# Attention and gated experts on one core: another way through the first 256 tokens of batch 0

## The chip, the cores and the metric

The kernel runs on one core of a Trainium2 chip. Its engines work in parallel, each through its own queue in order: PE (TensorE, matrix products and transposes), DVE (VectorE), ACT (ScalarE), POOL (GpSimd) and SP (SyncE, which here issues nearly all DMAs). The metric is the device time of one execution in microseconds, as the median of several runs.

## What is computed

Eight batches of 576 tokens go through a windowed attention with 8 heads of 64, and the result through a layer of four experts that are attention heads themselves.

```python
rel = pos[:, None] - pos[None, :]
mask = (rel >= 0) & (rel < 128)
scores = np.where(mask, q @ k.T / 8 - slope[h] * abs(rel), -1e9)   # per batch and head
x = softmax(scores) @ v                                            # (8, 576, 512)
...
logits = x @ w_gate                                                # 4 experts, the best 2 are kept
for e in range(4):
    q, k, v = x @ wq[e], x @ wk[e], x @ wv[e]                      # 512 -> 64
    ye = softmax(causal(q @ k.T / 8)) @ v @ wo[e]
    out += (weight of e per token, 0 if not among the best 2) * ye
```

## The kernel before

The heads are taken two at a time: a pair has 128 rows, head 0 of the pair in partitions 0 to 63 and head 1 in 64 to 127. In batch 0 the pairs are called g = 0 to 3. A key block is 128 keys wide, and since the window is 128, a block of 128 queries sees its own key block and the one ahead of it.

**Wrapped scores.** For query block i the kernel computes 256 scores per query (`products`), of which the mask leaves exactly 128, and folds them: where a key of the own block lies in the future, the score of the same column in the block ahead is copied over it (`wrap`, COPY_PREDICATED on DVE with the mask `mkt`). The softmax then works on 128 columns (`softmax_block` on DVE, shown as CUSTOM_DVE_ANT_0 or ISA; `exp_block` on ACT; `normalise` by `scl`, on POOL or ACT). After the transposes on PE, `split` (DVE, TENSOR_TENSOR with `tmt`) spreads the 128 columns again over two key blocks, one masked out for each entry, and PE multiplies by the values (`half_pv`).

**Batch 0 in halves.** The first batch is the start of the program, where nothing else is to be done. Its pairs are therefore worked in halves: half A (`x == 0`) is query blocks 0 and 1 of each pair, half B is blocks 2 and 3 and, by `half_tail`, the last 64 tokens. `half_s` makes scores and softmax, `half_t` the transposes, `half_pv` the product with the values. It leaves each x in two parts, `xh` (rounded to the type that PE takes in one pass) and `xl` (what the rounding left), in the tiles `wx`. `fetch(g, m, x)` brings only the part of q and k that a half needs, in pieces of 64 partitions x 2 x 256 (128 KB), the rest for half B later with other sources (`rd`).

**Weights.** `wload(c)` fetches 128x772 of the joined weights, `wprep(c)` rounds them into `WH` and puts the rest into `WL`. Every projection (`qkproj`, `vproj`) is the sum of three products for each of four pairs: WH by xh, WH by xl, WL by xh.

**What sets the order.** The whole program is first recorded as a list. `plan` then puts it in the order that the table `ORDER` gives, a long compressed string of numbers, and `nc.any` leaves the table the choice between two engines for copies, roundings and scalings. `place` gives out the buffers by that order: eight PSUM banks `ps`, and in SBUF eight of `w5` (w50 to w57), three of `w10` (w100 to w102) and four of `w4` (w40 to w43). An engine works its queue strictly in order, so an instruction that waits holds up all that stand behind it on the same engine. All compute instructions come from one line, L1189.

Of the kernel before, what the change touches and what calls it, by code (L numbers as in the profile page):

```python
# [10 lines left out]
F32 = mybir.dt.float32  # L11
# [9 lines left out]
DM = H * D  # L21
# [9 lines left out]
BIG = 3.0e38  # L31
EPS = 1e-9
# [6 lines left out]
    "c-p;KeOO#sdB69bckVgKy_*?3v(C6PEBMS*Xc<c?bfFFvTIT7{9onHn1q&8jMnfAOVI35@ObZH?C_IHND7cB6)I>p{5*sSG@RU@dpu{B=Y_N$2g{NSHCKf"  # L39
    "6vY18-Id*=f-Yd`+z<zw#Lk8|GhzQ6bP{@x>q!mqqZIPsVeKYrOmGCYuFQ>%z-v8K{;h(b;Yo><!;<0MQmKgl4wblhq4x~Nh`ed(9xr+Q%|MU6nTiZGR#Z"  # L40
    "7iPxD*~#vIGGwEmPQ9aSsJs_AHUGCP}W}wETDQ)B1~=}&#Lq+yHpktsz@cXQCc6ORm?4aWJCUU#^8l_?ziudJWAZ&%sn)ub$`b*yz8`8vE}BG_JdXMusb-"
    "_LvrcPz*^=+Q*-n*tX%E31QzE??nQ6G{A6)p0ono+`TqQ}Ebzd4q>QgW$6oi`u@mcWhYz0rG9~OWcR>__Q?}BcE`VH^%wa7NJGh{}*LNcb#r-hQI1SJXD@"
    "%}@?-z19r}`|)!^OPGw!CwtMR=M;m~9H0ak(c!JI+!UovE;8Qk%nE&~$#}qJ^-D@_XKeIcEO^yc0qmfHeLfEn-&HM;FW!aB&3Y7=Q{z&=o4{^;Sb2^*IYX"
    "h1AJXoq1V#R<OIki7)M@tD(HCAYo>h@M!b3;N$_Afl2<`F?Myi+*PzQVqx=nFdQllK$hRvGwhnZUo(6;pjecd6JL7ZyleHW`qQW_)#vX9#Y0n$KjVM?qvh"
    "=ohWOD1XFBlLQu{|A*l7v*=m;a!#uT;zA%K4MDn7EeR8cbSFAliQ6xvevp%9<|^8I)tIL_YwsSo!3=DR+e>8F+9YSxbzRSI60O6}loQQOS7F0-58e(pX0q"
    "*AJy5g{3`{l<28O?Hbh`?}AcHxM)BBJ6FS>$Y`wo{yw5=LjKor=K=QoB2JGH$DL&5^)6V#ACJCQ=R9QW?a?9S87rr&Ff@smNQOv4P6V0y1r%g%vS(Z!b@)"
    "-4-buoVe-H#{}HQ!X|<%3%#1fwltLK}dZ!itH9@2#2z9mfZh%xL`j{%zqOj`#a{v!J+v*zBsnEHZxkBB@+9t&^WMNijv8p!OpK^Qd!j+jt!ft=(yEo6lbv"
    "TXBECd~maBX(9X>53Gtv*n^1);J~ruKTo^6=96hhYmupyp-|X(MdS`|D4+gBQ*YncL5%V^-RGm^(zRRTSuZ|8Ub6of@Cm+s8Mvl<1eg6meA`Lgq_T0hV9_"
    "Hem~6jW_XxkG`}5=g&-6=fZ{)!Of55ryl$KXIEFVa<lReKxrb)JJ-qT;=<QfM}H64!M@|MFJAe?r!3h4wSc|mgj&j)x`w{$Gj*E5Y&ENdq+1Gsdc4pB{X_"
    "le+$w<4>tW(v7=);+cH_=gv@KXx)!-<8ph3O%EMbhWE||h^v)2p#BtY1`-ZQmM$I5(5_sXW)<fWd`e&%H5iY<D6<oubuP*&7;al2z~f2VE@SS5SYQ`xo;z"  # L50
# [192 lines left out]
def attn_moe_kernel(ctx, tc, hd, rd, vd, wall, wo, mk, tb, tm, mt, ident, out):  # L243
# [1033 lines left out]
```

## Time and profile before

| | us |
|---|---|
| median of 3 runs | 477.76 (477.13 to 478.05) |
| the profiled execution | 478.22 |
| its span, first to last instruction | 476.4 |
| PE busy | 468.2 (98%) |
| DVE busy | 410.3 (86%) |
| ACT busy | 371.0 (78%) |
| POOL busy | 218.2 (46%) |

The ends of matrix products are modelled, so that PE is shown busy also where its products follow each other loosely. The mean granted clock of PE is 0.996; it was lower only between 10 and 15 us, at 0.66. Of the chain of work that ended last, PE holds 80% of the span, DVE 8%, DMA 4%, ACT 3%.

### The profile page before, as it was taken

The numbers are of one execution on the slowest core, as the hardware profiler recorded it, in microseconds if no ns is written. First come the engines' busy times: TensorE is split into PE (matmuls) and PEld (weight loads), VectorE is DVE, ScalarE is ACT, GpSimd is POOL, SyncE is SP. The second block draws the span as 40 slices with busy tenths as digits, with TensorE's granted clock in tenths as the row PEclk, the third lists the DMA queues.
The fourth block names the chain that finished last, engine by engine and source line by source line (L and its number), as shares of the span: only waits on it lengthen the run. The fifth ranks groups of instructions, "written<-read, shape, count | busy, mean of one in ns | idle before, by whom it ended". The sixth has DMA issues, their size and how long they took to land.

```text
span 476.4 us, 17537 instructions
## 1 busy us (share of the span) xinstructions
PE 468.2 (98%) x6380; PEld 409.5 (86%) x6380; DVE 410.3 (86%) x1900; ACT 371.0 (78%) x1416; POOL 218.2 (46%) x451
## 2 busy tenths in 40 slices
PE   7999999999999999999999999999999999999996
PEld 5888889897889788798898988998889897899875
DVE  6899999989998998879979898898998979975840
ACT  5867978978989577797987989498786968934962
POOL 4713779093826227243381626625163613352440
PEclk9899999999999999999999999999999999999999
DMA  8889333009136026160362047411733030300033
GB/s 200 263 206 225 89 110 80 7 2 221 49 104 141 2 68 192 34 161 1 87 174 68 1 116 192 119 27 38 167 94 102 4 85 2 119 1 1 3 111 111
DMA packets 29861, 44.98 MB, mean 94 GB/s; under 512 B 9424, under 2 KB 15824, under 8 KB 29776
## 3 DMA queue, kind: packets, MB, share of 16 engines
q1 hardware_dynamic: 29040, 43.42, 34.3%
q8 instruction: 50, 0.82, 0.7%
q10 hardware_dynamic: 736, 0.46, 0.4%
q14 instruction: 35, 0.29, 0.2%
HBM read 34.42 MB, written 9.44 MB: 92 GB/s over the span
## 4 chain that ended last, share of the span: by engine, by line
PE 80%; DVE 8%; DMA 4%; ACT 3%; SPq 2%; POOL 2%; issue 1%; DVEq 0%
PE ps L1189 80%; DVE w L1189 5%; ACT w L1189 2%; SPq L1189 2%; POOL w L1189 2%; DMA w<-in_hd 2%; DMA w<-in_rd 1%; DVE ps L1189 1%; DMA w<-in_wall 1%; DVE KKm L1189 0%; DVE r L1189 0%; DVE WL L1189 0%; DVE ALm L1189 0%; DVE mr L1189 0%; ACT QJm L1189 0%
## 5 line engine op out<-in xcount | busy, mean ns | idle before, releaser
L1189 ACT COPY w<-ps 128x512 f32<-128x512 f32 (+3 forms) x230 | 92.9, 449 | 31.1 <-PE ps L1189 20.1
L1189 PE MATMUL ps<-wx,WH 128*128 128x288 f32 (+2 forms) x512 | 110.6, 300 | 0.0
L1189 ACT ACTIVATE w<-w,nm 128x128 f32<-128x128 f32 x252 | 98.8, 395 | 7.5 <-DVE nm L1189 7.3
L1189 POOL TENSOR_SCALAR w<-w,r 128x128 f32<-128x128 f32 x165 | 60.6, 380 | 88.5 <-ACT w L1189 30.5
L1189 POOL TENSOR_SCALAR w<-w,mr,w 128x256 f32<-128x256 f32 (+3 forms) x128 | 78.2, 621 | 43.0 <-DVE mr L1189 15.8
L1189 PEld LDWEIGHTS ps<-wx,WH 128*128 128x128 f32 x512 | 83.3, 189 | 1.5 <-DVE mnm L1189 0.2
L1189 ACT ACTIVATE w<-w,mnm 128x256 f32<-128x256 f32 (+3 forms) x128 | 70.9, 557 | 14.4 <-DVE mnm L1189 13.0
L1189 DVE CUSTOM_DVE_ANT_0 w<-ps,tbt 128x128 f32<-128x128 f32 x288 | 72.5, 283 | 2.9 <-PE ps L1189 2.1
L1189 DVE TENSOR_TENSOR w<-ps,tmt 128x768 f32<-128x768 f32 (+3 forms) x96 | 72.4, 771 | 2.0 <-PE ps L1189 0.9
L1189 PE MATMUL ps<-wx,WL 128*128 128x288 f32 (+2 forms) x256 | 72.0, 296 | 0.0
L1189 PE MATMUL ps<-WH,wx 128*128 128x260 f32 x288 | 62.9, 287 | 0.0
L1189 PE MATMUL ps<-idt,w 64*128 64x64 f32 (+1 forms) x1152 | 60.4, 231 | 1.3 <-POOL w L1189 1.0
L1189 PE MATMUL ps<-w 64*64 64x192 f32 (+3 forms) x1256 | 58.9, 306 | 0.5 <-DMA w<-in_hd 0.4
L1189 PEld LDWEIGHTS ps<-idt,w 64*128 64x128 f32 (+1 forms) x1152 | 48.1, 139 | 11.4 <-issue 3.7
L1189 PE MATMUL ps<-w,vt 64*64 64x192 f32 (+4 forms) x1344 | 56.6, 284 | 0.4 <-ACT w L1189 0.4
L1189 PEld LDWEIGHTS ps<-w,vt 64*64 64x64 f32 (+1 forms) x1344 | 49.7, 133 | 6.5 <-ACT w L1189 1.0
L1189 DVE COPY_PREDICATED ps<-mkt,ps 128x128 f32<-128x128 int32 (+2 forms) x160 | 50.0, 329 | 2.4 <-PE ps L1189 2.0
L1189 PEld LDWEIGHTS ps<-w 64*64 64x64 f32 (+1 forms) x1256 | 45.0, 134 | 7.8 <-DMA w<-in_hd 1.6
L1189 DVE CUSTOM_DVE_ANT_0 w<-ps,mtt 128x384 f32<-128x384 f32 (+2 forms) x96 | 49.8, 551 | 1.0 <-PE ps L1189 0.6
L1189 PEld LDWEIGHTS ps<-WH,wx 128*128 128x128 f32 x288 | 48.4, 190 | 0.7 <-DVE nm L1189 0.2
L1189 PE MATMUL ps<-w,w 128*64 128x64 f32 (+4 forms) x576 | 48.2, 319 | 0.0
L1189 ACT ACTIVATION_READ_ACCUMULATOR w<-w,nm 128x1 f32 x252 | 48.2, 191 | 0.0
(110 smaller groups left out, 944.9 us busy)
## 6 DMA issues: line engine op xcount, KB each, us to landing
w<-in_hd SPq DMA_DIRECT2D x56, 288.0 KB, 4.7
vt<-in_vd SPq DMA_DIRECT2D x28, 320.0 KB, 4.3
out<-w SPq DMA_DIRECT2D x31, 256.0 KB, 2.7
w<-in_hd SPq DMA_DIRECT2D x14, 128.0 KB, 3.6
w<-in_hd SPq DMA_DIRECT2D x56, 32.0 KB, 3.9
w<-in_wall SPq DMA_DIRECT2D x4, 386.0 KB, 5.5
out<-w SPq DMA_DIRECT2D x8, 128.0 KB, 2.3
vt<-in_vd SPq DMA_DIRECT2D x4, 192.0 KB, 4.8
```

The source lines that it names most:

```text
L1189: getattr(getattr(tc.nc, e), m)(*a, **k)
```

## The change

- **Fetches.** Each pair of batch 0 now comes in two DMAs of 64 partitions x 1216 (304 KB each), q and k whole for both halves; the first pair's second one is issued by ACT. `rd` is no longer read. `tmt` and the low part of `mkt` move from ACT's queue to SP's, behind weights and values. The tail's q comes by `fetch_tl`, one 128x128 DMA for each pair.
- **Half A without wrap.** `first_blocks` gives query block 0 its 128 scores and block 1 all its 256, side by side. The softmax of block 1 runs over 256 columns, there is no COPY_PREDICATED and no `split`. The bias for it is a new table FT, made at the start by two instructions on DVE and four on POOL, in the memory of the tile `KKm`, which is free until the first key projection. The three blocks of each head are transposed (6 instead of 4 transposes per pair) and copied out by two copies of 128x384.
- **Weights.** `wprep` rounds and subtracts in two pieces, 512 and 260 columns. The products with `WL` come last in the first projections (`terms`).
- **Tail scores of the batches after the first.** The two 64x128 and the two 64x64 products trade their rows; the fold then goes into the other bank. The number of instructions is the same.
- **A new `ORDER`** for the whole program. Counted over the program: PE 4794 instructions before, 4800 after; DVE 1902 and 1891; ACT 976 and 963; POOL 456 and 485; SP 241 and 238.

```diff
-    "c-p;KeOO#sdB69bckVgKy_*?3v(C6PEBMS*Xc<c?bfFFvTIT7{9onHn1q&8jMnfAOVI35@ObZH?C_IHND7cB6)I>p{5*sSG@RU@dpu{B=Y_N$2g{NSHCKf"
...
+    def fetch(g):
+        if g % 2 == 0:
+            raws["e", g // 2] = big10.tile([P, 2 * (QW + S)], F32, tag="e", name=f"e{g}")
+        z = (QW + S) * (g % 2)
+        e = raws["e", g // 2][:, z : z + QW + S]
+        a = hd[0, NP_ - 1 - g]
+        nc.sync.dma_start(e[:D], a[:D, : QW + S])
+        (nc.sync if g else nc.scalar).dma_start(e[D:], a[D:, QW + S + P :])
+        raws[g] = ([e[:, : NQ * P], e[:, P:QW]], e[:, QW:])
...
+    def first_blocks(g, ss, q, k, tb):
+        nm, sm, pt = state[g, 0]
+        for i in range(2):
+            n = P + P * i
+            for h in range(2):
+                d = slice(D * h, D * h + D)
+                for y in range(2):
+                    m = P * i + D * y
+                    nc.tensor.matmul(
+                        ss[h][D * y : D * y + D, P * i : P * i + n], q[h][d, m : m + D], k[d, :n], start=True, stop=True
+                    )
+        for h in range(2):
+            for i in range(2):
+                c = 2 * h + i
+                a = ss[h][:, : 3 * P].rearrange("p (a n) -> p a n", n=P)[:, i : 2 * i + 1, :]
+                v = pt[:, 3 * h + i : 3 * h + 2 * i + 1, :]
+                bias = tb[:, h, 1 - i :, :].bitcast(F32)
+                softmax_block(a, v, bias, nm[:, c : c + 1], P + P * i)
+                exp_block(None, v, nm[:, c : c + 1], sm[:, c, 0:1], P + P * i)
...
         if x == 0:
-            evac(w[:, : 4 * P].rearrange("p (h n) -> p h n", h=2)[:, :, :P], t[:, 0:2, :], 2 * P)
-            split(diag_pair(w, 1, 1, P), t[:, 2:4, :], P)
...
+            for h in range(2):
+                t = ps_t.tile([P, 4, P], F32, tag="t", name=f"tA{g}_{h}")
+                for k in range(3):
+                    nc.tensor.transpose(t[:, k, :], pt[:, 3 * h + k, :], idt)
+                evac(w[:, 3 * P * h : 3 * P * h + 3 * P].rearrange("p (a n) -> p a n", n=P), t[:, :3, :])
...
+    def terms(late):
+        return sorted(((c, j) for c in range(4) for j in range(3)), key=lambda z: late and z[1] == 2)
...
-            for lhs, rhs in ((WH, xh), (WH, xl), (WL, xh)):
...
+            lhs, rhs = ((WH, xh), (WH, xl), (WL, xh))[j]
...
+            for f in (slice(0, 4 * P), slice(4 * P, NW)):
+                w, hi, lo = wst[c][:, f], WH[:, NP_ - 1 - c, f], WL[:, NP_ - 1 - c, f]
+                rnd(hi, w)
+                ssub(lo, w, hi.bitcast(F32))
...
+    nc.vector.tensor_scalar(FT[:, 3, :, 0, :], tbt[:, 3, 0:3:2], -1.0e6, NEG, op0=ALU.is_ge, op1=mul)
+    nc.vector.tensor_tensor(FT[:, 3, :, 0, :], FT[:, 3, :, 0, :].bitcast(F32), tbt[:, 3, 1:4:2], add)
+    nc.gpsimd.tensor_scalar(FT[:, 3, :, 1, :], tbt[:, 3, 0:3:2], 1.0, 0.0, op0=mul, op1=add)
+    for p in (2, 1, 0):
+        nc.gpsimd.tensor_scalar(FT[:, p], FT[:, 3].bitcast(F32), float(4 ** (3 - p)), 0.0, op0=mul, op1=add)
```

The order on SP at the start of the program. `w100` holds pairs 0 and 1, `w101` pairs 2 and 3; `in_wall` are the weights, `in_vd` the values. Before:

```order
L1189 DMA w100_90<-in_hd 64x2x256 x4
L1189 DMA w101_91<-in_hd 64x2x256 x4
L1189 DMA w100_90<-in_hd 128x2x128
L1189 DMA w100_90<-in_rd 128x2x320
L1189 DMA w100_90<-in_hd 64x2x256 x2
L1189 DMA w51_83<-in_wall 128x772
L1189 DMA vt0_128<-in_vd 128x256
L1189 DMA vt1_129<-in_vd 128x256
L1189 DMA w55_87<-in_wall 128x772
L1189 DMA vt2_130<-in_vd 128x256
L1189 DMA vt3_131<-in_vd 128x256
```

The same place now (ACT issues one more 64x1216 for w100 beside it):

```order
L1189 DMA w100_90<-in_hd 64x1216 x3
L1189 DMA w101_91<-in_hd 64x1216 x2
L1189 DMA w51_83<-in_wall 128x772
L1189 DMA w101_91<-in_hd 64x1216 x2
L1189 DMA vt0_128<-in_vd 128x256
L1189 DMA w52_84<-in_hd 128x128
L1189 DMA vt1_129<-in_vd 128x256
L1189 DMA w53_85<-in_hd 128x128
L1189 DMA mkt_107<-in_mk 128x64
L1189 DMA w54_86<-in_wall 128x772
L1189 DMA vt2_130<-in_vd 128x256
L1189 DMA vt3_131<-in_vd 128x256
```

Before, the half A of all four pairs (eight pieces of 128 KB) and four DMAs for half B of pairs 0 and 1 stood ahead of the first weights; now the whole rows of pairs 0 to 2 do, pair 3 follows the first weights, and all values stand behind pair 3.

The order on DVE, from the last blocks of pair 2 in half A (`nmA2`) to the first of pair 3 (`nmA3`); `nm` names the pair and half of a softmax block, KKm is the table FT. Before:

```order
L1189 TENSOR_REDUCE r1_0_135<-sm1_116 128x4
L1189 RECIPROCAL r1_0_135<-r1_0_135 128x4
L1189 ISA w52_84,nmA2_136<-ps4_73,tbt_108 128x128
L1189 ISA nmA2_136 128x1
L1189 COPY_PREDICATED ps5_74<-mkt_107,ps5_74 128x128
L1189 ISA w52_84,nmA3_138<-ps5_74,tbt_108 128x128
L1189 ISA nmA3_138 128x1
L1189 COPY_PREDICATED ps6_75<-mkt_107,ps6_75 128x128
L1189 ISA w52_84,nmA3_138<-ps5_74,tbt_108 128x128
```

The same place now:

```order
L1189 TENSOR_REDUCE r1_0_135<-sm1_116 128x4
L1189 ISA w57_89,nmA2_136<-ps6_75,KKm_125 128x128
L1189 ISA nmA2_136 128x1
L1189 COPY_PREDICATED ps4_73<-mkt_107,ps4_73 128x2x128
L1189 RECIPROCAL r1_0_135<-r1_0_135 128x4
L1189 COPY_PREDICATED ps5_74<-mkt_107,ps5_74 128x2x128
L1189 TENSOR_TENSOR WL_112<-w51_83,WH_111 128x512
L1189 ISA w50_82,nmA3_138<-ps7_76,KKm_125 128x256
L1189 ISA nmA3_138 128x1
L1189 TENSOR_REDUCE r2_0_137<-sm0_115 128x4
L1189 ISA w50_82,nmA3_138<-ps7_76,KKm_125 128x128
```

Between the two pairs there now stand three COPY_PREDICATED for half B of pairs 0 and 1 and a subtraction for WL; pair 3's blocks of half A stand ahead of every softmax block of half B (`tbt` in place of KKm), which follow a few rows later.

The order on POOL from the scalings of pair 2's half A to the last part of WL. Before:

```order
L1189 TENSOR_SCALAR w52_84<-w52_84,r2_0_137 128x128 x2
L1189 TENSOR_SCALAR w52_84<-w52_84,r3_0_139 128x128
L1189 TENSOR_SCALAR w52_84<-w52_84,r2_0_137 128x128
L1189 TENSOR_SCALAR WH_111<-w51_83 128x772
L1189 TENSOR_TENSOR WL_112<-w51_83,WH_111 128x772
L1189 TENSOR_SCALAR WH_111<-w55_87 128x772
L1189 TENSOR_TENSOR WL_112<-w55_87,WH_111 128x772
L1189 TENSOR_SCALAR w53_85<-w53_85,r0_4_141 128x128
L1189 TENSOR_SCALAR WH_111<-w56_88 128x772
L1189 TENSOR_SCALAR w54_86<-w54_86,r1_4_143 128x128
L1189 TENSOR_SCALAR WH_111<-w57_89 128x772
```

The same place now (`r0_4` and `r1_4` are half B of pairs 0 and 1; w51, w54 and w57 hold the raw weights):

```order
L1189 TENSOR_SCALAR w50_82<-w50_82,r3_0_139 128x128
L1189 TENSOR_SCALAR w50_82<-w50_82,r3_0_139 128x256
L1189 TENSOR_SCALAR WH_111<-w54_86 128x512
L1189 TENSOR_SCALAR WH_111<-w54_86 128x260
L1189 TENSOR_TENSOR WL_112<-w54_86,WH_111 128x512
L1189 TENSOR_SCALAR w52_84<-w52_84,r0_4_141 128x128 x4
L1189 TENSOR_SCALAR WH_111<-w51_83 128x512
L1189 TENSOR_TENSOR WL_112<-w51_83,WH_111 128x512
L1189 TENSOR_SCALAR w53_85<-w53_85,r1_4_143 128x128 x4
L1189 TENSOR_TENSOR WL_112<-w57_89,WH_111 128x512
L1189 TENSOR_TENSOR WL_112<-w51_83,WH_111 128x260
L1189 TENSOR_TENSOR WL_112<-w57_89,WH_111 128x260
```

Before, POOL made two of the four WL and DVE the other two; now POOL makes three of the four 512-wide pieces, the last two of them each behind four scalings of half B, and three of the four 260-wide ones.

## Rows read from the trace of the kernel before

**Rows 1.** Stretches of 20 us: PE, PEld, DVE, ACT, POOL busy (instructions), clock, DMA share, GB/s
```profile
0.00:20.00 20.00, 17.39 (x161) 13.47 (x161) 14.39 (x92) 13.07 (x55) 11.62 (x24) 0.91 0.92 254
20.00:40.00 20.00, 19.83 (x240) 17.15 (x238) 19.39 (x87) 13.43 (x60) 6.36 (x14) 1.00 0.80 192
40.00:60.00 20.00, 19.95 (x330) 17.61 (x329) 19.35 (x100) 17.92 (x80) 11.46 (x24) 1.00 0.59 146
...
420.00:440.00 20.00, 20.00 (x189) 19.79 (x189) 11.52 (x46) 6.14 (x20) 8.58 (x20) 1.00 0.00 1
```

**Rows 2.** Chain that ended last, in order of time: start us, us, what
```profile
25.02 26.80 PE ps L1189 x380
51.83 0.27 ACT w L1189
...
65.29 0.28 ACT w L1189
...
66.17 43.24 PE ps L1189 x626
```

**Rows 3.** Timeline of the first 28 us: start, us, engine, operation [idle before, releaser]
```profile
4.80 0.90 PE L1189 MATMUL ps<-w 64*64 64x192 f32 x16
...
8.72 0.52 PEld L1189 LDWEIGHTS ps<-w 64*64 64x64 f32 x12 [0.37 <-DMA w<-in_hd]
...
18.37 0.38 PE L1189 MATMUL ps<-WH,wx 128*128 128x260 f32 x1
...
22.80 0.71 DVE L1189 TENSOR_TENSOR wx<-ps,wx 128x256 fp32r<-128x256 f32 x2
23.43 1.53 DVE L1189 TENSOR_TENSOR WL<-w,WH 128x772 fp32r<-128x772 f32 x1
...
25.02 0.50 PE L1189 MATMUL ps<-WL,wx 128*128 128x260 f32 x2 [0.17 <-DVE WL L1189]
...
27.37 0.49 PE L1189 MATMUL ps<-w 128*128 128x192 f32 x2
```

**Rows 4.** Instructions on DVE in the first 70 us, by form: count | busy us, mean ns
```profile
L1189 DVE CUSTOM_DVE_ANT_0 w<-ps,tbt 128x128 f32<-128x128 f32 x72 | 17.4, 281 | 2.3 <-PE ps L1189 2.1
...
L1189 DVE TENSOR_TENSOR w<-ps,tmt 128x1024 f32<-128x1024 f32 x4 | 4.9, 1216 | 0.0
L1189 DVE COPY_PREDICATED ps<-mkt,ps 128x128 f32<-128x128 int32 x16 | 4.3, 288 | 0.3 <-PE ps L1189 0.3
...
L1189 DVE TENSOR_TENSOR w<-ps,tmt 128x512 f32<-128x512 f32 x4 | 2.7, 683 | 0.4 <-ACT w L1189 0.4
L1189 DVE TENSOR_TENSOR WL<-w,WH 128x772 fp32r<-128x772 f32 x2 | 2.5, 1238 | 0.0
...
L1189 DVE CUSTOM_DVE_ANT_0 w<-ps,mtt 128x256 f32<-128x256 f32 x2 | 0.8, 422 | 0.0
```

**Rows 5.** Stretches: the last two numbers are the DMA engines' busy share and GB/s
```profile
1.00:2.00 1.00, 0.70 (x3) 0.70 (x4) 1.00 (x6) 0.00 (x0) 0.25 (x1) 1.00 0.27 41
...
3.00:9.00 6.00, 5.58 (x69) 3.98 (x70) 3.32 (x27) 3.85 (x14) 2.20 (x3) 1.00 1.04 222
15.00:18.00 3.00, 3.00 (x44) 2.26 (x38) 2.20 (x13) 1.85 (x9) 2.92 (x4) 1.00 1.03 379
109.00:116.00 7.00, 7.00 (x126) 5.27 (x126) 7.00 (x28) 5.26 (x21) 3.69 (x4) 1.00 1.05 242
```

**Rows 6.** DMA issues: queue, operation xcount, KB each, median us from issue to landing
```profile
w<-in_hd SPq DMA_DIRECT2D x14, 128.0 KB, 3.6
...
w<-in_wall SPq DMA_DIRECT2D x4, 386.0 KB, 5.5
...
tbt<-in_tb ACTq DMA_DIRECT2D x1, 160.0 KB, 2.5
```

**Rows 7.** Timeline of POOL at the start: start, us, operation [idle before, releaser]
```profile
9.05 2.83 POOL L1189 TENSOR_SCALAR w<-w,r 128x128 f32<-128x128 f32 x8 [3.42 <-DVE nmA L1189]
...
15.38 0.83 POOL L1189 TENSOR_SCALAR WH<-w 128x772 fp32r<-128x772 f32 x1
16.29 1.83 POOL L1189 TENSOR_TENSOR WL<-w,WH 128x772 fp32r<-128x772 f32 x1
```

More of the change, by code (lines that the diff above doesn't have):

```diff
@@ L31 @@
 BIG = 3.0e38
+NEG = -8.0e9
 EPS = 1e-9
@@ L499, in half_s, with first_norm @@
             ss = [ps_s.tile([P, 512], F32, tag="s", name=f"s{'AB'[x]}{g}_{h}") for h in range(2)]
-        part = products(ss, 2 * x, [q, q], k, tbt[:, p], 2, 5 * x)
+        if x == 0:
+            first_blocks(g, ss, q, k, FT[:, NP_ - 1 - g])
+            return
+        part = products(ss, 2, q, k, tb, 2, 5)
         for h in range(2):
-            wrap(ss[h], 2 * x)
-            blocks((g, x), ss[h], part[h])
+            wrap(ss[h], 2)
+            blocks((g, 1), ss[h], part[h])
+    def first_blocks(g, ss, q, k, tb):
[17 more added lines that the diff above has]
+                exp_block(None, v, nm[:, c : c + 1], sm[:, c, 0:1], P + P * i)
+    def first_norm(g):
+        nm, sm, pt = state[g, 0]
+        r = p2.tile([P, 5], F32, tag="r", name=f"r{g}_0", bufs=3)[:, :4]
+        nc.vector.tensor_reduce(r, sm[:, 0:4, :], AX.X, add)
+        nc.vector.reciprocal(r, r)
+        for c in range(4):
+            h, i = divmod(c, 2)
+            v = pt[:, 3 * h + i : 3 * h + 2 * i + 1, :]
+            scl(v, v, r[:, c : c + 1])
     def half_tail(g):
         s = ps_a.tile([P, 512], F32, tag="a", name=f"sC{g}")
-        nc.tensor.matmul(s[:, :TW], *prepped[g][4][2:4], start=True, stop=True)
+        nc.tensor.matmul(s[:, :TW], half["p", g][:, 0, :], prepped[g][4][1][:, S - TW :], start=True, stop=True)
         nc.vector.copy_predicated(s[:, 0:TAIL], mkt[:, P:], s[:, P:TW])
@@ L739, in qkproj @@
         o = acc[:, :n]
-        k = 0
-        for c in range(4):
+        for k, (c, j) in enumerate(terms(b == 0 and half == 0)):
             xh, xl = xT[4 * b + c]
             cw = c if b else NP_ - 1 - c
-            for lhs, rhs in ((WH, xh), (WH, xl), (WL, xh)):
-                nc.tensor.matmul(
-                    o, lhs[:, cw, P * mtile : P * (mtile + 1)], rhs[:, n0:n1], start=(k == 0), stop=(k == 11)
-                )
-                k += 1
+            lhs, rhs = ((WH, xh), (WH, xl), (WL, xh))[j]
+            nc.tensor.matmul(
+                o, lhs[:, cw, P * mtile : P * (mtile + 1)], rhs[:, n0:n1], start=(k == 0), stop=(k == 11)
+            )
         sl = slice(n0, n1)
@@ L1102, in attn_moe_kernel @@
     warm()
-    fetch(1, 1, 0)
+    for g in range(1, 4):
+        fetch(g)
     fetch_v(0, 0)
-    fetch(2, 2, 0)
     fetch_v(1, 0)
+    wload(0)
     fetch_v(2, 0)
-    wload(0)
     fetch_v(3, 0)
```

279 lines of the change are left out of this document (114 added, 165 removed).

## The prediction

> **What bounds the kernel now.** I read the stretches of 20 us first, then the chain, then the timeline of the start, where the change lies. Between 20 and 60 us DVE is busy 19.39 and 19.35 of 20 us, while PE, shown as busy, has its products less densely: in 420 to 440 us DVE needs only 11.52 of 20 us and PE's weight loads fill 19.79, against 17.15 and 17.61 [rows 1]. So in the first 60 us DVE is as good as full, and later PE is. The chain says the same with a seam: it runs on PE from 25.02 us, leaves it at 51.83 us for ACT and DVE until 65.6 us (13.8 us), and returns to PE at 66.17 us [rows 2]. What the start costs, DVE decides together with what arrives when: scores begin at 4.80 us, the last pair's half A at 8.72 us, the first projection at 18.37 us; the last two `xl` leave DVE at 22.80 to 23.51 us, DVE then makes WL from 23.43 us on, PE waits for it at 25.02 us, and these projections end at 27.37 us [rows 3]. After that PE always has something to do. So the change can gain in two ways: an earlier end of this first part, and less DVE work in the part up to 65 us.
>
> **DVE's work.** Out go eight COPY_PREDICATED 128x128 of 0.288 us (2.3 us), four `split` 128x512 of 0.683 us (2.7 us), and two WL of 772 columns, 1.238 us each (2.5 us), for which one piece of 512 and one of 260 come back: as many columns as one, 1.2 us. In come eight softmax blocks of 256 columns in place of 128: 8 x (0.422 - 0.281) = 1.1 us; three of the eight copies 128x384, between 0.42 us (256 columns) and 0.68 us (512), say 0.55 us: 1.7 us; two instructions for FT over 256 columns, 0.8 us. Sum: -2.3 - 2.7 - 1.3 + 1.1 + 1.7 + 0.8 = **-2.7 us** of DVE time [rows 4]. Its other copies trade engines in the new order by less than 1 us net. PE gets eight more transposes and 16 wider products, under 1 us, all in the first 20 us, where it waits anyway; ACT gets eight exponentials of twice the width and five of the copies, and has room there (busy 13.07 and 13.43 of 20 us [rows 1]).
>
> **The fetches.** A whole pair is two pieces of 304 KB where half A needed two of 128 KB. What rate do they get? In 3 to 9 us, when the 64-partition pieces of 1 KB rows came in, the DMA engines were fully busy at 222 GB/s; in 15 to 18 us, mostly weights over 128 partitions, they moved 379 GB/s; in 109 to 116 us, where the large pieces are 64 partitions again, with rows of 2.3 and 4.6 KB, 242 GB/s [rows 5]. Long rows therefore don't help; the number of partitions goes with the rate, and I take 242. [...]
>
> Ahead of pair 3's scores lie the table of 160 KB, the identity (128x128, 64 KB), eight pieces of 64x1216 (304 KB each; 2656 KB in all, 2.72 MB) and one weight piece of 386 KB [rows 6]. Data flows from about 2 us: in 1 to 2 us the DMA engines are busy 0.27 [rows 5]. 2.72 MB at 242 GB/s are 11.2 us, the weights at 379 another 1.0 us: pair 3 lands at **14.3 us**, and the first values 0.4 us later. At 222 it is 15.3 us, at 379 it would be 10.2 us. Before, the last scores of half A began at 8.72 us. So the whole-row fetch itself makes half A later, not earlier; pairs 0 and 1 have their half B scores in exchange.
>
> **The first part, after pair 3.** DVE's queue holds every half-B block behind pair 3's blocks. From these to the last `xl` DVE has: 2 blocks of 256 and 13 of 128 (4.5 us), three copies (1.7), four subtractions and two casts of 256 (2.5), a `split` of 256 (0.4), a WL of 260 (0.4), some nine small ones (1.6): 11.1 us. Neighbours overlap: two subtractions of 0.42 us take 0.71 us together [rows 3], so of 34 instructions about 2 us go off. 14.3 + 9.1 gives 23.4 us for the last `xl`; before it was 23.51. DVE then stands even on the x, but has already done what it did before up to about 26 us (no WL, no second half of the weights), which is the 2.7 us above.
>
> Now the end of the projections. DVE makes pair 1's half-B sums only after a `split` of 128x1024, 1.22 us [rows 4], so near 25.0 us. POOL then has four scalings (8 in 2.83 us, 1.4 us) and the last WL of 512 (1.83 us x 512 / 772 = 1.2 us) [rows 7]: 27.6 us, and four products follow on PE: **28.1 us** where before it was 27.4. By then PE has also made the half-B scores of pairs 2 and 3 and more transposes, but fewer projections; about the same work: 19 projections of 256 to 260 columns less, against 16 score products of 192 in two passes (two side by side), two tails and five transposes. So this part costs 0.7 us; with pair 3 one us earlier or later, between -1.5 and +2 us.
>
> **After it.** DVE is ahead by 2.7 - 0.7 = 2.0 us of its old place. What of it the end sees: nothing, if PE alone decided between 28 and 65 us; all, if DVE did. DVE is idle 1.3 us of 40 there, and the chain lies on ACT and DVE for 13.8 us of it; I take nine tenths, 1.8 us. From 66 us on PE is the bound, its work is the same, and the new order moves it by chance only, which I bound by 1.5 us each way (the DVE and ACT stretch of the chain is one such place; a new order can open or close a few like it).
>
> **Sum.** +0.7 - 1.8 = -1.1 us. The profiled execution took 478.22 us (span 476.4, 1.8 us around it), so 477.1; it lies 0.46 us above the median of the runs, 477.76, and there the sum gives **476.7 us**.
>
> **Rivals.** (a) *The start gains too.* Halves of different partitions in flight together (ACT's piece beside SP's) could reach a rate nearer to 379 GB/s. Then pair 3 lands 2 us earlier, DVE has no gap ahead of it, and the first part ends at 26.1 us: 1.3 us gained there and 1.8 us after: 474.7 us or less. For it: the two queues at the start; against it: pieces of both halves alternate in 3 to 9 and 109 to 116 us too, at 222 and 242. Chance 0.2. (b) *DVE's relief buys nothing*, since PE was the bound from 25 us on, as most of the chain says, and the 0.7 us are hidden by products that don't wait: 477.8 us. Chance 0.25. (c) *Slower: pair 3 holds all queues.* Its scores stand on PE ahead of the first product with the values, its blocks on DVE ahead of half B. If it lands at 16 us or later (210 GB/s or less), each us goes through DVE's sums, POOL's scalings and the last WL to PE: at 16.5 us the first part ends at 30.3 us, 2.9 us late, of which DVE's 1.8 us cancel a part: 478.9 us; where the relief buys nothing either, 480.7. For it: 222 in the first 9 us. Against it: 242 on pieces of like size. It decides from a landing at 15.4 us on, where the loss (0.7 + 1.1 us) is what DVE gives back. Chance 0.2. (d) *The change does less than it says*: half A without wrap saves DVE 2.7 us, but the copies could all wait on ACT; that is within (b).
>
> **How the numbers follow.** The forecast, 476.7 us, has 0.35. Its own range is 475.2 to 478.2 by the 1.5 us of the later order. A measurement of this kernel can tell about 0.2% from no change, 0.96 us, so faster means below 476.8 us and slower above 478.7. Of the forecast 0.22 lies below, 0.11 within, 0.02 above; of (a) 0.2 below; of (b) 0.05 below, 0.15 within, 0.05 above; of (c) 0.04 within and 0.16 above. That is 0.47 faster, 0.30 same, 0.23 slower. The range reaches to (a), 474.7 less 1 us for the order, and to the middle of (c): 473.7 to 479.9 us.
>
> **What would show it.** In the new profile: the scores of the last pair (64x256 on PE, the second use of w101) start at 14 to 15 us; nearer to 11 us is (a), beyond 16 us (c). The two WL pieces of 512 on POOL at 24 and 26 to 28 us, and PE waiting for POOL ahead of its last products of the first projections, near 28 us. DVE less than 19 of 20 us busy in 40 to 60 us, if the relief is there, and the chain on PE between 50 and 66 us; if DVE is as full as before, the relief went elsewhere. I am wrong if the DMA rate in 3 to 12 us is over 300 GB/s, or if PE stays dense from before 25 us on.

## The result: 480.5 us, slower, by the third rival and by a fetch that the prediction passed over

The changed kernel takes 480.53 us (median of 8 runs, 478.62 to 484.10), the kernel before, on the same chips, 476.71 (476.43 to 478.05): a ratio of 1.0077, 95% interval 1.0050 to 1.0105. The forecast was 476.7 us, the range ended at 479.9, and slower had a chance of 0.23. The forecast counted from 477.76 us; against 476.71 its -1.1 us would be 475.6, and +3.8 was measured. The profiled execution is the slowest of the eight, 484.1 us with a span of 482.3; where its start is not typical, an experiment with the same start is set beside it.

The timeline of PE in the changed kernel (start, us, engine, line, operation, in brackets the idle time ahead of it and what ended it), against [rows 3]:

```profile
4.59 0.68 PE L1189 MATMUL ps<-w 64*64 64x128 f32 x4
8.41 4.90 PE L1189 MATMUL ps<-w 64*64 64x128 f32 x64 [3.14 <-DMA w<-in_hd]
...
17.15 0.65 PE L1189 MATMUL ps<-w 64*64 64x256 f32 x4 [1.97 <-DMA w<-in_hd]
18.84 1.55 PE L1189 MATMUL ps<-w 64*64 64x256 f32 x12 [1.05 <-DMA w<-in_hd]
...
26.50 0.61 PE L1189 MATMUL ps<-wx,WH 128*128 128x256 f32 x3
```

Pair 0's lower rows are there at 4.6 us, its upper ones at 8.4 us. Pair 3 comes at 17.15 us (lower) and 18.84 us (upper); the prediction had 14.3. The first projection follows at 26.50 us, where before it stood at 18.37. The stretches (PE, PEld, DVE, ACT, POOL busy, granted clock, DMA share, GB/s) against [rows 1] and [rows 5]:

```profile
0.00:20.00 20.00, 12.28 (x116) 9.05 (x116) 9.22 (x53) 8.06 (x27) 10.03 (x22) 0.88 0.88 206
40.00:60.00 20.00, 20.00 (x322) 18.10 (x318) 19.33 (x104) 14.93 (x69) 8.65 (x25) 1.00 0.86 196
60.00:80.00 20.00, 17.62 (x240) 15.55 (x241) 17.02 (x70) 13.43 (x54) 15.28 (x32) 1.00 0.23 73
...
3.00:9.00 6.00, 2.86 (x20) 1.89 (x19) 1.00 (x9) 0.65 (x1) 4.51 (x7) 0.96 0.94 241
8.00:14.00 6.00, 5.34 (x74) 3.85 (x76) 3.37 (x19) 3.67 (x14) 1.55 (x5) 0.72 1.05 223
15.00:18.00 3.00, 0.82 (x6) 0.22 (x4) 2.16 (x12) 2.37 (x10) 2.58 (x5) 1.00 1.08 210
```

In the first 20 us DVE does 9.22 us of work, where it did 14.39, and PE 12.28, where it did 17.39: they wait for data. Meanwhile the DMA engines are busy without a gap and move 210 to 241 GB/s. And there is a second hole, in 60 to 80 us, where PE works 17.62 us. The chain that ended last shows both (start, us, what):

```profile
1.16 7.20 DMA w<-in_hd
8.38 10.33 DMA w<-in_hd
18.84 27.44 PE ps L1189 x268
...
56.69 6.33 DMA w<-in_wo
...
67.64 2.38 POOL WOL L1189
70.05 0.62 DVE w L1189 x2
70.72 191.62 PE ps L1189 x2635
```

The second hole is the fetch of `wo`. In the new order it stands on SP behind all loads of the rows for pairs 4 to 10, is issued at 56.69 us and lands 6.3 us later; POOL, in order, waits 3.59 us for it ahead of WOH, then makes the copies to `QJm` and WOL late; DVE waits for WOL, and PE for DVE, 2.38 us, from 68.3 to 70.7 us:

```profile
63.18 1.05 POOL L1189 TENSOR_SCALAR WOH<-w 128x1024 fp32r<-128x1024 f32 x1 [3.59 <-DMA w<-in_wo]
...
70.72 0.56 PE L1189 MATMUL ps<-wx,WH 128*128 128x320 f32 x2 [2.38 <-DVE w L1189]
```

### The profile page after: what moved, and what is told of

It is laid out like the page before. It is cut to its first block, busy times and chain, and to the rows that moved or that the text cites. A ratio compares the mean times of both kernels' runs of the same rounds, so it can differ in the third digit from the quotient of the medians.

```text
span 482.3 us, 17570 instructions
## 1 busy us (share of the span) xinstructions
PE 467.3 (97%) x6386; PEld 406.8 (84%) x6386; DVE 408.7 (85%) x1889; ACT 371.2 (77%) x1404; POOL 229.1 (48%) x480
## 4 chain that ended last, share of the span: by engine, by line
PE 82%; DMA 6%; DVE 3%; POOL 3%; ACT 3%; SPq 1%; issue 1%; ACTq 0%; DVEq 0%; POOLq 0%
PE ps L1189 82%; DMA w<-in_hd 5%; ACT w L1189 2%; POOL w L1189 2%; DVE w L1189 2%; SPq L1189 1%; DMA w<-in_wo 1%; DVE ps L1189 1%; POOL WOL L1189 0%; POOL QJm L1189 0%; DVE wx L1189 0%; DVE mr L1189 0%; DVE ALm L1189 0%; ACT AHm L1189 0%; ACT wx L1189 0%
## 5 line engine op out<-in xcount | busy, mean ns | idle before, releaser
L1189 ACT COPY w<-ps 128x512 f32<-128x512 f32 (+4 forms) x236 | 94.5, 446 | 28.6 <-PE ps L1189 22.6
L1189 POOL TENSOR_SCALAR w<-w,r 128x128 f32<-128x128 f32 (+1 forms) x178 | 66.8, 390 | 80.1 <-ACT w L1189 30.8
L1189 DVE TENSOR_TENSOR w<-ps,tmt 128x768 f32<-128x768 f32 (+2 forms) x92 | 69.8, 775 | 4.6 <-PE ps L1189 3.2
L1189 PE MATMUL ps<-wx,WL 128*128 128x288 f32 (+2 forms) x256 | 69.3, 295 | 0.0
L1189 DVE CUSTOM_DVE_ANT_0 w<-ps,tbt 128x128 f32<-128x128 f32 x272 | 67.6, 283 | 0.7
L1189 PE MATMUL ps<-WH,wx 128*128 128x260 f32 x288 | 60.1, 286 | 0.2 <-DVE w L1189 0.2
L1189 PEld LDWEIGHTS ps<-w 64*64 64x64 f32 x1248 | 43.6, 136 | 14.6 <-DMA w<-in_hd 4.2
L1189 DVE CUSTOM_DVE_ANT_0 w<-ps,mtt 128x512 f32<-128x512 f32 (+2 forms) x96 | 50.0, 551 | 1.3 <-PE ps L1189 1.0
L1189 PE MATMUL ps<-w,w 128*64 128x64 f32 (+5 forms) x584 | 50.4, 320 | 0.0
L1189 DVE COPY_PREDICATED ps<-mkt,ps 128x128 f32<-128x128 int32 (+2 forms) x152 | 47.5, 332 | 2.5 <-PE ps L1189 2.0
```

What stands on the lines that cost most here:

```text
L1189: getattr(getattr(tc.nc, e), m)(*a, **k)
```

## Experiments

Each kernel was timed in turn with the kernel before (medians 476.85, 477.05, 477.10 and 476.89 us in the four groups: e1 to e4; e5 to e8; e9, e10 and e12; e13). "Scores" is the start of pair 3's last scores (of all its scores, where they run without a gap), "first" that of the first projection, both in the profiled run. The runs of the new kernels spread by 2.4 to 5.5 us, so a difference of two medians below is good to about 1 to 1.5 us (95%, from the spread and the number of runs).

| kernel | edit | median us (runs) | ratio to before, 95% | scores | first |
|---|---|---|---|---|---|
| changed | | 480.53 (8) | 1.0050 to 1.0105 | 18.84 | 26.50 |
| e1 | wo early | 478.91 (12) | 1.0024 to 1.0060 | 17.30 | 21.98 |
| e2 | column pieces | 477.67 (12) | 0.9995 to 1.0031 | 14.33 | 20.41 |
| e3 | pair 0 all on SP | 478.76 (12) | 1.0024 to 1.0048 | 15.88 | 20.55 |
| e4 | half A first | 479.26 (6) | 1.0029 to 1.0068 | 14.07 | 20.15 |
| e5 | changed + fillers | 482.67 (6) | 1.0088 to 1.0128 | 20.20 | 24.89 |
| e6 | e3 + wo early | 477.79 (12) | 0.9991 to 1.0029 | 16.87 | 21.55 |
| e7 | e2 + wo early | **474.82** (6) | 0.9922 to 0.9965 | 14.10 | 20.18 |
| e8 | e6 + 3.9 us of DVE | 479.37 (7) | 1.0031 to 1.0072 | 15.27 | 20.72 |
| e9 | e7, pair 3 late | 479.99 (6) | 1.0047 to 1.0080 | 17.70 | 24.23 |
| e10 | e7 + 3.9 us of DVE | 476.67 (11) | 0.9972 to 0.9998 | 13.27 | 19.37 |
| e12 | e7, pair 0 all on SP | 474.84 (6) | 0.9930 to 0.9968 | 12.44 | 18.54 |
| e13 | e9 + fillers | 478.36 (12) | 1.0018 to 1.0051 | 17.54 | 22.40 |

**e1, wo early.** The table of numbers sets SP's order; only the place of six fetches in it is changed:

```diff
 SP, behind the first loads of r6, r7 and r8 (r10 is the rows of pair 10):
-  five fetches of r10, among 13 more of r6 to r9; vt6; wo; vt5 ...
+  wo; the 13 of r6 to r9; vt6; five fetches of r10; vt5 ...
```

> The changed kernel with one thing moved: the fetch of wo stands in SP's queue where the five fetches of r10 stood (ahead of the bulk of the loads), and these stand where wo stood. Theory A (wo's late fetch is a loss of its own): WOH on POOL no longer waits 3.59 us for it, the 2.38 us that PE waits for DVE at 70.72 us go, and the time is 480.5 - 2.4 = 478.1 us, the start unchanged (pair 3's upper piece near 18.8 us). Theory B (only the start counts): what comes after is late anyway, 480.0 to 481.0 us. Theory C (SP's loads decide there): r10 is now late and another wait of 2 us or more opens, 480.5 us or slower.

478.91 us, 1.6 less than the changed kernel. POOL no longer waits, and PE has no wait in 55 to 80 us (timeline of POOL, then a piece of the chain, both of e1):

```profile
56.06 1.04 POOL L1187 TENSOR_SCALAR WOH<-w 128x1024 fp32r<-128x1024 f32 x1
```
```profile
47.96 70.47 PE ps L1187 x993
```

The time lies between the theories, nearer to A's 478.1 than to B's 480.0, and the waits went as A had it: a late `wo` costs something of its own. The start is untouched by the edit, and shows the second surprise: here pair 3's last scores begin at 17.30 us, and only 4.7 us pass to the first projection, where the changed kernel's profiled run needed 7.7 (18.84 to 26.50). The difference goes with the clock: it stayed at 1.00 in e1, though PE waited there for 3.28 us ahead of pair 0's upper scores, while in the changed kernel's profiled run it was 0.50 from 19 to 25 us, right behind PE's waits of 1.97 and 1.05 us, and pair 3's twelve scores took 1.55 us, where the twelve at 13.50 us, at a clock of 1.00, took 0.87 (stretches of the changed kernel):

```profile
15.00:19.00 4.00, 0.98 (x10) 0.41 (x12) 2.16 (x12) 2.37 (x10) 3.16 (x6) 0.97 1.02 222
19.00:25.00 6.00, 6.00 (x33) 4.57 (x33) 3.58 (x23) 3.11 (x12) 2.54 (x6) 0.50 0.45 104
```

**e2, column pieces.** `h0` holds batch 0's two needed row halves under one another, so that a piece spans 128 partitions; bytes, queues and number of transfers stay. `h0` is one more input array, joined ahead of the kernel.

```diff
-        a = hd[0, NP_ - 1 - g]
-        nc.sync.dma_start(e[:D], a[:D, : QW + S])
-        (nc.sync if g else nc.scalar).dma_start(e[D:], a[D:, QW + S + P :])
+        a = h0[NP_ - 1 - g]
+        nc.sync.dma_start(e[:, :QW], a[:, :QW])
+        (nc.sync if g else nc.scalar).dma_start(e[:, QW:], a[:, QW:])
```

> The changed kernel with the pieces of a pair cut by columns: 128 partitions x 640 (q) and 128 x 576 (k) from an array that holds both halves, in place of two pieces of 64 partitions x 1216; the same bytes, queues, order and number of transfers. Theory A (64 partitions set the rate, 210 to 242 GB/s, where 128 reached 379): pair 3's last piece lands near 12 us in place of 18.84, the first projection is 6 us earlier, and with two thirds of that left at the end the time is 476 to 477 us. Theory B (the queues and the issue order set it, whatever the partitions): pair 0's second piece still lands near 8.4 us and pair 3 near 17 to 19 us, and the time is 480 to 481 us.

Theory A for the fetches: the DMA engines, as full as before, move 376 and 369 GB/s instead of 241 and 223, a piece (320 or 288 KB now) lands after 5.2 us in place of 9.1 for 304 KB, PE no longer waits for pair 3's data, and the first projection is 6.1 us earlier (stretches, then DMA issues of e2, then of the changed kernel):

```profile
3.00:9.00 6.00, 4.10 (x34) 3.26 (x37) 2.05 (x17) 1.44 (x6) 3.43 (x6) 1.00 1.01 376
8.00:14.00 6.00, 6.00 (x76) 5.19 (x70) 3.83 (x23) 4.12 (x17) 4.58 (x9) 1.00 1.05 369
```
```profile
w<-in_h SPq DMA_DIRECT2D x4, 320.0 KB, 5.2
```
```profile
w<-in_hd SPq DMA_DIRECT2D x7, 304.0 KB, 9.1
...
w<-in_hd ACTq DMA_DIRECT2D x1, 304.0 KB, 7.2
```

477.67 us is 0.7 above the 476 to 477 expected; `wo` is still late here, and the wait for it, 2.1 us at 64 to 66 us, is followed by a clock of 0.73 and then 0.50:

```profile
64.00:66.00 2.00, 0.00 (x0) 0.00 (x0) 0.57 (x3) 0.00 (x0) 2.00 (x2) 1.00 0.15 58
66.00:68.00 2.00, 1.91 (x18) 1.56 (x20) 2.00 (x13) 1.33 (x6) 2.00 (x6) 0.73 0.00 0
68.00:70.00 2.00, 2.00 (x20) 1.80 (x18) 1.92 (x4) 0.63 (x4) 2.00 (x7) 0.50 0.00 0
```

**e3, pair 0 all on SP.**

```diff
-        (nc.sync if g else nc.scalar).dma_start(e[D:], a[D:, QW + S + P :])
+        nc.sync.dma_start(e[D:], a[D:, QW + S + P :])
```

> The changed kernel with pair 0's upper piece issued by SP instead of ACT; nothing else. Theory A (ACT's piece is starved beside SP's stream, and SP's later issues wait for it): pair 0's scores start near 5.5 us in place of 8.41, pair 3's second piece is issued some 2 us earlier and lands near 16 us; 478 to 479.5 us. Theory B (the total rate decides): pair 0 starts early but pair 3 still lands at 18 to 19 us, and the time stays at 480 to 481 us.

478.76 us, 1.8 less than the changed kernel: theory A. The reason lies on SP. In the changed kernel (first) its two issues of pair 3 take 4.04 us, in e3 (second) 1.12:

```profile
0.73 3.18 SPq L1189 DMA_DIRECT2D w<-in_hd  x5
...
4.80 4.04 SPq L1189 DMA_DIRECT2D w<-in_hd  x2
8.89 0.59 SPq L1189 DMA_DIRECT2D vt<-in_vd  x1
```
```profile
5.18 1.12 SPq L1189 DMA_DIRECT2D w<-in_hd  x2
```

Five issues before them take 3.18 us. SP's waits in the first 10 us of the changed kernel have one of 3.0 us, for a DMA of `in_hd`, so the second of the two was held until about 8.4 us, when ACT's piece landed (1.16 us and 7.20 in the chain above). That it was ACT's piece which SP waited for is inferred from that coincidence and from the 1.12 us in e3:

```profile
SPq L1189 <- DMA w<-in_hd: 3.0, 1, 3.0
```

**e4, half A first.** `h0` as in e2; each pair is a piece of 2 x 384 columns with all that half A needs, and two with the rest; the four first pieces stand ahead.

```diff
 SP: -  p0 p0(ACT) p1 p1 p2 p2 wall0 p3 p3 vt0 ...
     +  p0a p1a p2a p3a p0b p0c p1b p1c wall0 p2b p2c p3b p3c vt0 ...
```

> The changed kernel with the fetches of all four pairs over 128 partitions, and what half A needs first: one piece of 2 x 384 columns for each pair, then two pieces with the rest of each. All on SP. Theory A (the landing of pair 3's half A is the price of the change): it lands near 7.5 us, the first products with the values start near 11 us in place of 20.3, the first projections end 7 to 9 us earlier, and two thirds of that is left at the end: 475 to 476.5 us, level with the kernel before or faster. Theory B (the new order is worse by itself, the start is hidden by later waits): 479 to 481 us although pair 3 lands early.

The time is in theory B's range, but neither mechanism is shown. Pair 3's scores begin at 14.07 us without a wait for data, as in e2, since PE's order has the half B scores of pairs 0 and 1 ahead of them; so with this order an earlier landing of its half A buys nothing. Why its median is 1.6 us above e2's is not settled: its profiled run (477.59 us, the lowest of six) is not slower, and four of the six had a mean clock of 0.991 or less.

**e5, fillers in the changed kernel.** 12, 8 and 4 products on `QJm` that nobody reads, ahead of pair 0's upper, pair 3's lower and pair 3's upper scores.

> The changed kernel with idle PE given work that nobody reads: 12 filler products of 256 columns (as in its first 3.4 us) ahead of pair 0's upper scores, 8 ahead of pair 3's lower and 4 ahead of pair 3's upper scores; the fetches are untouched. Theory A (the lower clock that follows the waits is a loss of its own: granted clock 0.50 in 9 to 12 and 19 to 25 us of the changed kernel's profile): the clock stays at 1.00 up to 30 us, the first projection comes near 22 us as in the draw with wo early, and the median is 478.5 to 479.5 us with less spread. Theory B (PE's clock there is hidden behind DVE, or the fillers only take the place of waiting): 480 to 481 us.

482.67 us, above both theories, and it doesn't decide. The clock did stay at 1.00 until 68 us. But a filler writes to a PSUM bank; from 16.4 us on the fillers waited for DVE and ACT, by these rows, and then stood ahead of pair 3's lower scores, which start behind them without a wait for data:

```profile
16.41 0.39 PE L1191 MATMUL ps<-QJm 128*128 128x256 f32 x1 [0.18 <-DVE nmA L1191]
17.02 0.38 PE L1191 MATMUL ps<-QJm 128*128 128x256 f32 x1 [0.23 <-DVE nmA L1191]
17.79 1.24 PE L1191 MATMUL ps<-QJm 128*128 128x256 f32 x6 [0.39 <-ACT w L1191]
18.95 0.65 PE L1191 MATMUL ps<-w 64*64 64x256 f32 x4
```

**e6 and e7: both losses undone.** e6 is e3 with e1's order, e7 is e2 with e1's order.

> The changed kernel with pair 0's upper piece on SP and wo's fetch in r10's place, the two edits that gave 478.76 and 478.91 us apart (changed kernel 480.53). Theory A (the losses at the start and at wo add up): 477.0 us, and no wait of PE over 1 us between 55 and 72 us. Theory B (the earlier start makes room in which wo's wait is hidden, or the other way round): no better than the better one alone, 478.5 us.

> The changed kernel with pieces cut by columns over 128 partitions, and wo's fetch in r10's place. Theory A (both losses add up, and the relief of DVE that the prediction counted on, 1.8 us, then shows): 475.5 to 476.2 us, faster than the kernel before (476.85). Theory B (DVE's relief buys nothing; only losses are undone): 476.5 to 477.5 us.

e7 takes 474.82 us: theory A, faster than both kernels, 0.9943 of the kernel before, and better than expected. Its chain (start, us, what) stays on PE where the changed kernel's left it:

```profile
17.11 90.99 PE ps L1187 x1238
```

e6's 477.79 lies between its theories and is level with the kernel before (ratio 0.9991 to 1.0029). e6 and e7 differ in two things, the partitions of a piece and the queue of pair 0's second; the pair that differs in the partitions alone is e6 and e12 (below), and it costs 2.95 us, for scores that are 4.4 us later. The place of `wo` is worth 1.6 us (changed to e1), 1.0 (e3 to e6, not clear of the spread) and 2.85 (e2 to e7).

**e8 and e10: DVE's work given back.** e6 and e7 with eight subtractions of 128x240 that nobody reads, two each at four places.

> The kernel with pair 0 on SP and wo early, and besides eight DVE subtractions of 240 columns that nobody reads, two each at four places between about 32 and 62 us: near 3 us of DVE's time given back. Theory A (DVE's work there is the bound, as the prediction had it: nine tenths of a saving reach the end): 2.5 us slower than the same kernel without them. Theory B (DVE's relief buys nothing): within 0.5 us of it.

> The kernel with column pieces and wo early (474.82 us), with eight DVE subtractions of 240 columns that nobody reads at four places in 30 to 50 us, which took 0.43 us each in the run with pair 0 on SP: 3.5 us of DVE's time. Theory A (DVE is the bound in 28 to 65 us, as the prediction had it): 0.9 x 3.5 us, 478.0 us. Theory B (PE is the bound there): 475.0 us. In between, the share of DVE's saving that reaches the end can be read off.

They ran from 29 to 48 us and took 3.9 us in all (e10, DVE by form):

```profile
L1191 DVE TENSOR_TENSOR dum<-WH,WL 128x240 f32<-128x240 f32 x8 | 3.9, 492 | 0.1
```

e10 is 1.85 us slower than e7, e8 1.6 us slower than e6: in between by the medians, 0.4 to 0.5 of DVE's time, with an uncertainty of over 1 us each. The two traces say more, since the start can be taken out. The order is the same in e7 and e10. Ahead of the first added subtraction e10's profiled run was 0.8 us early, behind the last it is 2.55 us late (e7, e10; e7, e10):

```profile
25.19 1.23 ACT L1187 CAST WH<-w 128x260 fp32r<-128x260 f32 x3
24.36 1.23 ACT L1191 CAST WH<-w 128x260 fp32r<-128x260 f32 x3
...
69.17 0.69 PE L1187 MATMUL ps<-KKm,QJm 128*128 128x288 f32 x4
71.72 0.70 PE L1191 MATMUL ps<-KKm,QJm 128*128 128x288 f32 x4
```

That is 3.4 us for 3.9, and of these 3.15 us are left at the end (474.35 and 476.67 us, and the 0.83 of the start). So between 0.4 and 0.9 of DVE's time there reaches the end: not nothing, and the prediction's 0.9 is not refuted.

**e9 and e13: pair 3 made late, with PE idle and with PE busy.** In e7's order pair 3's fetches are put behind vt0, vt1, the tail rows and the second weights, and behind three loads of 386 KB into a free buffer; e13 also puts 16 fillers ahead of pair 3's scores.

```diff
+    load = [("sync", "dma_start", (big10.real[2][:, NW * i : NW * i + NW], wall[:, i, :]), {}) for i in range(3)]
+    seq_ = [x for o in seq_ for x in (load + [o] if o is nc.ops[27] else [o])]
```

> The kernel with column pieces and wo early (474.82 us, pair 3's scores at 14.1 us without a wait for data), and pair 3's two fetches made late on purpose: they stand behind the first v, the tail rows and the second weight piece, and behind three transfers of 386 KB each that nobody reads. Pair 3 should land near 17 us. Theory A (what decides is when pair 3 lands, each us beyond some 14 to 15 us goes through to the end): 477.5 to 478.5 us. Theory B (a late pair 3 is caught up later, the loss of the changed kernel came from elsewhere): 475.0 to 476.0 us.

> The kernel whose pair 3 is late on purpose (scores at 17.7 us, 479.99 us; PE idle for 5.63 us before, granted clock 0.50 from about 15.6 to 22 us), with 16 filler products of 256 columns on PE ahead of pair 3's scores, so that PE waits busy; they end before the data lands. Theory A (a good part of a late landing's price is the lower clock after the idle time): the clock stays at 1.00, the first projection comes 2 to 3 us earlier than 24.23 us though pair 3 lands at the same 17.7 us, and the median is 477.5 to 478.5 us. Theory B (the price is the lateness itself): the first projection stays within 1 us, 479.5 to 480.5 us.

e9: 479.99 us, 5.2 us more than e7 for scores 3.6 us later; theory A, and more than it allowed. e13: 478.36, 1.6 us less than e9 with the data as late. PE's wait in e9, then stretches of e9, then of e13:

```profile
17.70 1.56 PE L1189 MATMUL ps<-w 64*64 64x256 f32 x16 [5.63 <-DMA w<-in_h]
```

```profile
16.00:18.00 2.00, 0.30 (x4) 0.33 (x8) 0.00 (x0) 0.00 (x0) 0.00 (x0) 0.50 0.86 281
18.00:20.00 2.00, 2.00 (x20) 1.10 (x16) 0.71 (x6) 0.19 (x1) 0.00 (x0) 0.50 0.07 21
20.00:22.00 2.00, 2.00 (x12) 1.57 (x9) 1.43 (x10) 2.00 (x9) 1.75 (x5) 0.50 0.00 0
```
```profile
16.00:18.00 2.00, 2.00 (x22) 1.78 (x25) 0.00 (x0) 0.10 (x2) 1.30 (x4) 1.00 0.94 326
18.00:20.00 2.00, 2.00 (x27) 1.48 (x20) 1.55 (x13) 1.02 (x5) 0.59 (x2) 1.00 0.12 37
20.00:22.00 2.00, 2.00 (x14) 1.30 (x15) 2.00 (x13) 2.00 (x9) 1.95 (x5) 1.00 0.00 0
```

From pair 3's scores to the first projection it is 6.5 us in e9 and 4.9 in e13. So the late landing has two prices: the lateness, 3.5 us for 3.4 (e7 to e13), and the clock behind the idle time, 1.6 by the medians and 0.9 by the two profiled runs (478.62 and 477.68 us). The three added loads also stand ahead of all that follows on SP, in both kernels; what part of the 3.5 us comes from that was not taken apart.

**e12, e7 with pair 0 all on SP.** As e3, on e7.

> The kernel with column pieces and wo early (474.82 us), with pair 0's second piece on SP too, right behind the first. Theory A (ACT's piece, which landed 5.0 us after its issue, still holds pair 0's scores): scores at 5 us in place of 6.33 and the end 0.5 to 1 us earlier, 474 us. Theory B (later links of the first part decide: the softmax blocks, the scalings and the last WL): 474.8 us unchanged.

474.84 us, theory B's figure, but six runs each can't tell it from the 0.5 to 1 us of theory A. The first projection comes 1.6 us earlier, at 18.54 us. A group of eight products that starts at 37.65 us in e7 starts at 36.59 in e12, so 0.6 of that is gone by then; PE waits on the way for the rows of the next pairs, 0.27 us. The rest is still there near the end (last copy on ACT in e7, then in e12):

```profile
469.10 0.37 ACT L1187 COPY w<-ps 128x256 f32<-128x256 f32 x1 [0.92 <-PE ps L1187]
468.11 0.37 ACT L1187 COPY w<-ps 128x256 f32<-128x256 f32 x1 [0.92 <-PE ps L1187]
```

The spans, 472.6 and 472.4 us, differ by 0.2 alone, and why was not followed. So an earlier start than e7's is worth 1.0 us up to there in these two runs; the medians show none of it.

## Why the prediction was wrong

**The fetches: the step that failed.** "I take 242" treated nine pieces as one stream in which pair 0 is on time, and gave 14.3 us. Two things were off. The rate: 223 GB/s in 8 to 14 us and 210 in 15 to 18; by the prediction's own sum 223 gives 15.2 us. And the queues, which the sum left out and rival (a) counted as a gain: ACT's piece took 7.2 us, and SP's issuing of pair 3 was held for 3.0 us until about the time when it landed. Undoing the second alone (e3) brings the last scores to 15.88 us, near that 15.2; in the changed kernel they came at 18.84 us, and in e1, with the same start, at 17.30. Why these two differ by 1.5 us stays open. The row that should have warned was among those shown: 222 GB/s in 3 to 9 us came from 64-partition pieces at the start, the case in question, and 242 from another part of the program [rows 5]. The prediction chose the higher of the two.

The changed kernel and e2 move the same bytes over 64 and over 128 partitions: 241 against 376 GB/s in 3 to 9 us and 223 against 369 in 8 to 14 us, ratios of 0.64 and 0.60. So the number of partitions went with the rate here too, as the prediction read it from the rows.

**The price of lateness.** Rival (c) had the mechanism and the place: pair 3 holds PE's and DVE's queues, from a landing of about 15 us on. It gave 478.9 us for 16.5 us. Put into its sum, the 17.30 us of e1 make +1.9 us; e1, whose `wo` is early, took 2.1 us more than the kernel before. Its other figure, 480.7 without any relief, lies by the measured 480.5 by luck, since that holds 1.6 us for `wo`, which no rival had. What (c) lacked is the lower clock while PE starts again, 0.50 in 16 to 22 us of e9 and worth 0.9 to 1.6 us there, and also part of the 3.0 us by which the changed kernel's profiled run, the slowest of its eight, was slower than e1 from the scores to the first projection.

**The fetch of wo: a term that was missing.** The prediction followed the order on SP for the first pairs only and put all that comes after 28 us into "chance only, 1.5 us each way". `wo` moved from 40 us behind the loads of seven pairs, which can be read from the order without running anything, and cost 1.0 to 2.9 us.

**DVE's relief: right in sign, its size open.** The single costs held in the changed kernel: 0.55 us for a copy of 384 columns, 0.68 and 0.39 us for the pieces of WL, 0.42 us for a block of 256. But the whole program's DVE time fell by 1.6 us (410.3 to 408.7), not 2.7, and of each us there 0.4 to 0.9 reaches the end: 0.7 to 2.4 us, where 1.8 were forecast. "DVE less than 19 of 20 us busy in 40 to 60" was a bad sign to watch: it is 19.33 us in the changed kernel and 19.59 in the faster e7, probably because later work moves up.

**The first part.** From pair 3's scores to the last `xl` on DVE the sum had 9.1 us. In e1 the last subtraction ends at 26.72 us, 9.4 us behind 17.30:

```profile
26.31 0.41 DVE L1187 TENSOR_TENSOR wx<-ps,wx 128x256 fp32r<-128x256 f32 x1
```

That step held. The next one had POOL's last WL, and the products behind it, end at 28.1 us, 13.8 behind pair 3's scores. In e1 these products end at 32.1 us, 14.8 behind, and without a wait for POOL: no row of PE's waits in the changed kernel or in e7 names WL, since other products stand ahead. Nor is it the same end as the 27.4 us of before. The 24 products of 260 columns that stood there up to 28.0 us now follow the scores of the next pair's rows; in e7 they run from 36.0 to 39.8 us (e1, then the last of them in e7):

```profile
31.14 1.00 PE L1187 MATMUL ps<-wx,WL 128*128 128x256 f32 x7
...
39.08 0.76 PE L1187 MATMUL ps<-WL,wx 128*128 128x260 f32 x5
```

The prediction set them against score products done earlier. So its +0.7 us, from 28.1 and 27.4, compares unlike ends, and no run shows that term by itself.

**The later order.** e7's first projection is 1.8 us later than before and its end 2.2 us earlier: 4.0 us are won behind it (a rough mark, since other work stands ahead of it now). DVE's relief is 0.7 to 2.4 of that; the rest, 1.6 us or more, exceeds the 1.5 us that the prediction allowed, and no run here takes it apart. With its fetches as they are but for the queue of one piece and the place of `wo` (e6), the change is level with the kernel before; with column pieces too (e7) it gains 2.2 us. The kernel before with column pieces was not run, so how much of these 2.2 us belongs to the change is not shown.

## What to carry to other kernels

Take the rate for a fetch from a row with the same number of partitions and the same place in the program, and cut a block by columns over all 128 partitions where the layout is yours: the same bytes came here at 369 instead of 223 GB/s. Where a table reorders a program, follow every queue for as long as the new order differs, and look above all for a transfer that has moved behind a bulk load, and for who waits for it. An early stage in which PE waits for data was paid for twice here: 3.5 us for a landing 3.4 us later (e7 to e13), and 0.9 to 1.6 us for the clock of 0.50 behind the wait (e9 against e13). Fillers helped where they ended about when the data came (e13, 1.6 us less than e9), and not where they stood ahead of data that had come (e5, 2.1 us more than the changed kernel).

## What was not expected of the hardware

- A piece of 304 KB on ACT's queue, issued at 1.16 us beside SP's stream, took 7.2 us to land, while SP's first piece, issued at 0.73 us, was used at 4.59 us; and SP, between two issues, waited 3.0 us until about 8.4 us (4.04 us for the two, 1.12 in e3, where that piece is issued by SP).
- The granted clock was 0.50 behind PE's idle times at the start of the changed kernel (3.14 us ahead of 9 to 11 us; 1.97 and 1.05 us ahead of 19 to 25 us) and of e9 (5.63 us; 16 to 22 us), and 0.73, then 0.50 behind a wait of 2.1 us in e2. It stayed at 1.00 behind 3.28 us at 8.6 us in e1 and behind 2.4 us at 70.7 us in the changed kernel. In the kernel before it was 0.66 from 10 to 15 us, though PE's longest idle time there was 0.74 us. So in these runs the length of one wait does not tell whether the clock falls. With fillers in the wait it stayed at 1.00 (e13).
- The spread of the runs goes partly with it: the kernel before varies by 1.6 us over its eight runs, the changed kernel by 5.5, with mean clocks of 0.989 (484.1 us) to 1.000 (479.2 and 479.6 us), though its fastest run, 478.62 us, had 0.996.
